# A long convolution's 16-point stages on row halves of the systolic array, and one output stored from another queue

## The chip, the cores and the metric

The kernel runs on one NeuronCore of a Trainium2 chip. The core has TensorE (PE, the 128x128 systolic array, which writes only to PSUM), VectorE (DVE), ScalarE (ACT), GpSimd (POOL) and SyncE (SP); SP, ACT and POOL also issue DMAs, each in its own order. The metric is the device time of one execution, in microseconds, the median of several. Whatever is called a weight load (PEld) is the loading of a matmul's stationary operand; the moving operand then streams through the array, one column after the other.

## The reference

The program computes a network of four residual layers on x = A_q (2048 positions, 448 channels) and the gradients of everything.

- Layer A, used twice: `x + n * (conv(kv) + kv * D)`, where n is the layer norm of x, `kv = shift(k) * v` with a causal 4-tap shift, and conv is a causal convolution of 2048 positions with one kernel per channel, which the reference does with an FFT of 4096 points.
- Layer B, used twice: `x + silu(norm(x) @ w1) @ w2`, with 1792 hidden units.
- The outputs: the result, and the gradients by A_q, k, v, the shift kernel, the long kernel (448x2048), D, w1 and w2. All in bf16.

kv does not depend on x, so the convolution is done once forwards, and its backward pass once, with the gradient that both layers A leave.

## The kernel before

**The convolution.** A position is n = 16 n1 + n2. Stage 1 is, for each of the 16 values of n2, a pair of matmuls (real and imaginary part) with a 128x128 table over n1 (`_fft_stage1`, line 198). Its result A1 has, for each frequency k1 on a partition, blocks of 128 columns, which hold 4 channels x 2 parts x 16 values of n2. Each block is transposed on TensorE (`turn`, line 350; line 1091 in the backward part), so that these 128 values lie on the partitions. Stage 2 (`_fft_stage2`, line 206) multiplies by a 128x128 matrix that holds a 16-point transform for each of the 4 channels. In the spectrum the product of two complex numbers is taken by two real products on DVE, one with a copy in which real and imaginary half have changed places (`_swap_halves` on DVE, `_swap_halves_dma` by two DMAs). The inverse (`_fft_inv_stage2_chunk`, line 216) takes a chunk of 8 blocks: for each block two matmuls of 128x128 by 128 columns, accumulated; this also turns the block back. Last, matmuls with the inverse table give the positions (lines 496, 1173, 1202). A spectrum has 14 chunks of 1024 columns, worked in pairs; "cp" counts the seven pairs.

**The order.** `_ssm_prefix` does the spectrum of the long kernel (K), then the convolution of kv: from about 5 to 101 us. K's spectrum stays on chip as `KAB` with its swapped copy, and is also stored to DRAM (`SPEC_d`), as is that of kv. `Main.run` does the layers forwards and backwards, in four blocks of 512 positions, to about 517 us. `_ssm_suffix` does the convolution's backward pass: stage 1 on the gradient (`_s1_gy`), the transposes, then `spectrum(cp)` and `inverse(cp)` in turn, each inverse twice, for the gradients of the kernel (`B1k`) and of kv (`B1v_`); then the gradients of v and k, the kernel gradient `gK` (lines 1194 to 1206) and that of the shift kernel (lines 1218 to 1233).

**Jobs.** The weight gradients of layer B are 56 products of 16 matmuls with 448 moving columns (class `Jobs`, line 950), cut into 224 steps of four matmuls. `jobs.run(n)` puts n steps into TensorE's program at that place. They fill TensorE while other engines prepare the next part of the convolution. `jobs.run(1000)` at the end does what is left; a result's transposes and store come one result later (`flush`, line 1028).

**What sets the order.** TensorE's order is the program's, by hand (`manual_schedule`). For the other engines a planner of the framework orders the instructions by its own estimates. `bal.pick` gives each eviction from PSUM to ACT or DVE by a running sum of estimated loads. PSUM is used in tagged rings: "mm" has two buffers of two banks in the main and backward part, "A" four such buffers in the prefix. The products `pa`, `pb` of the backward inverse lie in a ring of three (`pab`); `gK` has two buffers.

Of the kernel before, what the change touches and what calls it, by code (L numbers as in the profile page):

```python
# [17 lines left out]
P = 128  # L18
S = 2048
D = 448  # L20
# [8 lines left out]
NDH = D // 4  # L29
SPEC = NDH * P  # L30
# [3 lines left out]
def make_fft_consts():  # L34
# [10 lines left out]
    def qidx(m, c, ks):  # L45
        return 64 * c + 4 * m + ks
# [32 lines left out]
    GiBc = np.roll(GiBc, 64, axis=0)  # L79
# [118 lines left out]
def _fft_stage1(k, n2, rhs, A1, psum, m=None):  # L198
    nc = k.nc
    ps = psum.tile([P, 2, 512], FP32, name="ps_s1", **k.pt["s1"])  # L200
    for c in range(2):
        nc.tensor.matmul(ps[:, c, :D], lhsT=k.M1sb[:, n2 if m is None else m, c, :], rhs=rhs, start=True, stop=True)
    _copy(nc, k.bal.pick(2 * D), A1[:, :, :, n2, :].rearrange("p dh c ds -> p c dh ds"), ps[:, :, :D].rearrange("p c (dh ds) -> p c dh ds", ds=4))


def _fft_stage2(k, Zf, psum, consume, chunks, base=0):
    nc = k.nc
    for ci in chunks:
        ps = psum.tile([P, 1024], FP32, name="ps_s2", **k.pt["s2"])
        for hh in range(2):  # L210
            c0 = (ci - base) * 1024 + hh * 512
            nc.tensor.matmul(ps[:, hh * 512:(hh + 1) * 512], lhsT=k.Gsb[:, G_FWD, :], rhs=Zf[:, c0:c0 + 512], start=True, stop=True)
        consume(ci, ps)


def _fft_inv_stage2_chunk(k, pa, pb, conj, B1, ci, psum, cnd=False):
    nc = k.nc
    ga, gb = (G_IAC, G_IBC) if conj else (G_IA, G_IB)
    pv = psum.tile([P, 8, P], FP32, name="ps_v", **k.pt["v"])
    for i in range(8):  # L220
        nc.tensor.matmul(pv[:, i, :], lhsT=pa[:, i * P:(i + 1) * P], rhs=k.Gsb[:, ga, :], start=True, stop=False)  # L221
        nc.tensor.matmul(pv[:, i, :], lhsT=pb[:, i * P:(i + 1) * P], rhs=k.Gsb[:, gb, :], start=False, stop=True)  # L222
    if cnd:
        _copy(nc, k.bal.pick(1024), B1[:, :, 32 * ci:32 * ci + 32].rearrange("p q (dh ds) -> p dh q ds", ds=4),
              pv[:].rearrange("p dh (q ds) -> p dh q ds", ds=4))
    else:
        _copy(nc, k.bal.pick(1024), B1[:, 8 * ci:8 * ci + 8, :].rearrange("p a b -> p (a b)"), pv[:].rearrange("p a b -> p (a b)"))
# [7 lines left out]
def _swap_halves_dma(k, dst, src, lo, hi, eng, dlo=None):  # L235
    if dlo is None:
        dlo = lo
    dhi = dlo + (hi - lo)
    eng.dma_start(out=dst[0:64, dlo:dhi], in_=src[64:128, lo:hi])
    return eng.dma_start(out=dst[64:128, dlo:dhi], in_=src[0:64, lo:hi])  # L240
# [46 lines left out]
def _ssm_prefix(k):  # L287
# [4 lines left out]
    with ExitStack() as es:  # L292
# [8 lines left out]
        A1kv = k.mdp.tile([P, NDH, 2, 16, 4], BF16, name="A1kv", tag="DA")  # L301
        KAB = spec.tile([P, 2, SPEC], BF16, name="KAB")
        A1K = KAB[:, 0, :].rearrange("p (a c n s) -> p a c n s", c=2, n=16, s=4)
# [46 lines left out]
        def turn(src, dst, g):  # L350
            pt = psum.tile([P, 16, P], BF16, name="ps_tr", **a_)
            for i in range(16):
                nc.tensor.transpose(pt[:, i, :], src[:, 16 * g + i, :], k.ident[:])  # L353
            for lo, hi, o in dst(g):
                _copy(nc, bal.pick((hi - lo) * P, dve_ns=0.53), o, pt[:, lo:hi, :])
# [35 lines left out]
        def stage1_kv(h, jq, kvt):  # L391
            for u in range(0, 4, 2):
# [5 lines left out]
                for w in range(2):  # L398
                    _copy(nc, bal.pick(2 * DH), A1kv[:, 56 * h:56 * (h + 1), :, n2 + w, :].rearrange("p dh c ds -> p c dh ds"),
                          ps[:, w, :, :DH].rearrange("p c (dh ds) -> p c dh ds", ds=4))  # L400

        def cons_ka(ci, ps):
            sl = slice(ci * 1024, (ci + 1) * 1024)
            _copy(nc, bal.pick(1024), Ka[:, sl], ps[:])
            if ci % 2 == 1:
                lo, hi = (ci - 1) * 1024, (ci + 1) * 1024
                nc.gpsimd.dma_start(out=k.SPEC_d["K"][:, lo:hi], in_=Ka[:, lo:hi])
# [6 lines left out]
        for h in range(2):  # L414
            for i, jq in enumerate((1, 2, 3, 0)):
# [9 lines left out]
                else:  # L425
                    _fft_stage2(k, Ka, psum, cons_ka, range(2 * i, 2 * i + 2))
                    _swap_halves_dma(k, KAB[:, 0, :], Ka, 2048 * i, 2048 * i + 2048, nc.gpsimd)
# [6 lines left out]
        _fft_stage2(k, Ka, psum, cons_ka, range(8, NCI))  # L434
        for i in range(4, 7):
            _swap_halves_dma(k, KAB[:, 0, :], Ka, 2048 * i, 2048 * i + 2048, nc.gpsimd)

        B1 = A1kv[:].rearrange("p a c n s -> p a (c n s)")
# [8 lines left out]
        A1f = A1kv[:].rearrange("p a c n s -> p a (c n s)")  # L447
        for g in range(7):
            turn(A1f, zdst, g)
# [32 lines left out]
        for ci in range(NCI):  # L482
            _fft_stage2(k, zkv(ci * 1024, (ci + 1) * 1024), psum, cons_prod, (ci,), ci)
# [3 lines left out]
        B1v = B1.rearrange("p a (c n s) -> p a c n s", c=2, n=16)  # L487
        k.Ysb = k.wk.tile([P, J, D], BF16, name="Ysb", tag="W2")

    def ys():  # L490
        for i in range(8):
            py = k.psum.tile([P, 2, 512], FP32, name="ps_y", tag="mm", bufs=2)
            for u in range(2):
                n2 = 2 * i + u
                for c in range(2):
                    nc.tensor.matmul(py[:, u, :D].rearrange("p (dh ds) -> p dh ds", ds=4), lhsT=k.Minvsb[:, n2, c, :], rhs=B1v[:, :, c, n2, :], start=(c == 0), stop=(c == 1))
# [9 lines left out]
class Main:  # L506
# [257 lines left out]
    def run(self, ys):  # L764
# [57 lines left out]
        for c in range(4):  # L822
# [59 lines left out]
            else:  # L882
# [5 lines left out]
                k.A1g = k.mdp.tile([P, NDH, 2, 16, 4], BF16, name="A1g", tag="DA")  # L888
# [161 lines left out]
def _ssm_suffix(k):  # L1050
# [8 lines left out]
    with ExitStack() as es:  # L1059
# [28 lines left out]
        for g in range(7):  # L1088
            pt = psum.tile([P, 16, P], BF16, name="ps_tr", **mm)
            for i in range(16):  # L1090
                nc.tensor.transpose(pt[:, i, :], A1f[:, 16 * g + i, :], k.ident[:])
# [185 lines left out]
```

## Time and profile before

| what | time or share |
|---|---|
| runs before: median of 3 | 728.43 us (728.0 to 730.16) |
| the profiled execution's own time | 730.31 us |
| its span in the trace | 728.5 us |
| PE busy | 690.6 us, 95% |
| DVE busy | 472.7 us, 65% |
| ACT busy | 444.8 us, 61% |
| POOL busy | 98.1 us, 13% |
| inverse chunks, lines 221 and 222: matmuls | 336 + 336 |
| stage 2, lines 212 and 1103: matmuls | 56 + 28 |
| transposes, lines 353 and 1091: matmuls | 192 + 112 |

A row of the timeline gives the start, the length, the engine, the line, and how many equal instructions it joins; in brackets, how long the engine had been idle and what released it. The length of a joined row reaches from the first start to the last end, and ends of matmuls are modelled: a single matmul of 448 columns lasts 353 ns, but in a stream the next starts after 190 ns. So paces are taken from starts, and busy time per instruction is no pace. A row of the windows gives the start and end of the stretch, its length, then for PE, PEld, DVE, ACT and POOL the busy time and in brackets the instructions, then TensorE's granted clock, the busy share of the DMA engines and their GB/s.

### The profile page before, as it was taken

The numbers are of one execution on the slowest core, as the hardware profiler recorded it, in microseconds if no ns is written. First come the engines' busy times: TensorE is split into PE (matmuls) and PEld (weight loads), VectorE is DVE, ScalarE is ACT, GpSimd is POOL, SyncE is SP. The second block draws the span as 40 slices with busy tenths as digits, with TensorE's granted clock in tenths as the row PEclk, the third lists the DMA queues.
The fourth block names the chain that finished last, engine by engine and source line by source line (L and its number), as shares of the span: only waits on it lengthen the run. The fifth ranks groups of instructions, "written<-read, shape, count | busy, mean of one in ns | idle before, by whom it ended". The sixth has DMA issues, their size and how long they took to land.

```text
span 728.5 us, 12878 instructions
## 1 busy us (share of the span) xinstructions
PE 690.6 (95%) x5105; PEld 383.8 (53%) x5105; DVE 472.7 (65%) x1112; ACT 444.8 (61%) x545; POOL 98.1 (13%) x165
## 2 busy tenths in 40 slices
PE   6998799899999999999999999999899999999897
PEld 4876545454544444444444444545466666655654
DVE  4789843666879658898488845836764444449930
ACT  5888774578988858778587792135354445444311
POOL 1153110110010100101001000000102110013221
PEclk9999999999999999999999999999999999999999
DMA  9999946279939897197881999787648896568861
GB/s 316 261 286 327 373 110 167 91 175 258 273 108 223 227 237 195 48 242 229 229 205 38 228 249 345 190 215 191 228 159 328 302 358 242 155 185 275 292 211 48
DMA packets 192905, 160.64 MB, mean 220 GB/s; under 512 B 140619, under 2 KB 173134, under 8 KB 191948
## 3 DMA queue, kind: packets, MB, share of 16 engines
q1 hardware_dynamic: 178240, 111.14, 57.2%
q0 software_dynamic: 10896, 38.58, 15.1%
q10 hardware_dynamic: 3708, 10.09, 3.8%
q8 instruction: 40, 0.66, 0.4%
q14 instruction: 21, 0.17, 0.1%
HBM read 67.32 MB, written 54.60 MB: 167 GB/s over the span
## 4 chain that ended last, share of the span: by engine, by line
PE 65%; DVE 13%; issue 10%; ACT 7%; POOL 2%; DMA 2%; SPq 0%; DVEq 0%; ACTq 0%; POOLq 0%
PE ps_d L950 20%; PE ps_n L737 9%; PE ps_h L565 7%; PE ps_g L565 7%; PE ps_o L699 6%; PE ps_v L221 2%; PE ps_v L222 2%; POOL rstd L260 2%; PE ps_h L569 1%; PE ps_cv L381 1%; PE ps_g L569 1%; DVE n L262 1%; DVE pab L475 1%; PE ps_tr L353 1%; ACT KAB L111 1%
## 5 line engine op out<-in xcount | busy, mean ns | idle before, releaser
L950 PEld LDWEIGHTS <-dstat 128*128 128x128 bf16 x896 | 85.0, 98 | 73.5 <-issue 2.4
L737 PE MATMUL ps_n<-w1T,ghT 128*128 128x448 bf16 x448 | 95.0, 353 | 0.0
L699 PE MATMUL ps_o<-w2sb,aT 128*128 128x448 bf16 x448 | 89.9, 353 | 2.5 <-DVE X L703 2.5
L565 PE MATMUL ps_h<-nT,w1sb 128*128 128x512 bf16 (+1 forms) x420 | 84.8, 337 | 4.1 <-ACT Dall L111 2.4
L565 PE MATMUL ps_g<-nT,w2T 128*128 128x512 bf16 x336 | 79.7, 379 | 1.1 <-DVE Dall L112 0.6
L111 ACT CAST ghT<-ps_g 128x1024 bf16<-128x1024 f32 (+1 forms) x54 | 47.8, 903 | 53.3 <-PE ps_g L569 38.7
L737 PEld LDWEIGHTS <-ghT 128*128 128x128 bf16 x448 | 41.6, 98 | 44.6 <-issue 7.9
L699 PEld LDWEIGHTS <-aT 128*128 128x128 bf16 x448 | 43.0, 98 | 42.0 <-issue 5.0
L565 PEld LDWEIGHTS <-w1sb 128*128 128x128 bf16 x420 | 39.2, 98 | 40.4 <-issue 11.5
L682 ACT ACTIVATE aT<-ps_h 128x1024 bf16<-128x1024 f32 (+1 forms) x48 | 44.2, 921 | 20.6 <-PE ps_h L569 12.3
L898 DVE SCALAR_TENSOR_TENSOR lb_v<-lb_u,n 128x448 bf16<-128x448 bf16 x60 | 37.3, 621 | 28.9 <-ACT lb_u L741 28.4
L111 ACT CAST Dall<-ps_h 128x1024 bf16<-128x1024 f32 (+2 forms) x60 | 54.3, 904 | 0.0
L692 ACT ACTIVATE Dall<-Dall 128x1024 bf16<-128x1024 bf16 (+1 forms) x48 | 53.8, 1189 | 0.1
L565 PEld LDWEIGHTS <-w2T 128*128 128x128 bf16 x336 | 31.8, 98 | 38.2 <-issue 4.9
L260 POOL TENSOR_TENSOR rstd<-ln_ve,mhalf 128x2 f32<-128x2 f32 (+1 forms) x24 | 19.3, 805 | 222.9 <-DVE ln_ve L259 213.1
L950 PE MATMUL ps_d<-X,dstat 128*128 128x448 bf16 x224 | 48.4, 352 | 0.0
L950 PE MATMUL ps_d<-go,dstat 128*128 128x448 bf16 x224 | 48.1, 353 | 0.0
L950 PE MATMUL ps_d<-n3m,dstat 128*128 128x448 bf16 x224 | 48.1, 357 | 0.0
L950 PE MATMUL ps_d<-n1m,dstat 128*128 128x448 bf16 x224 | 47.3, 355 | 0.0
L221 PE MATMUL ps_v<-Gsb,pab 128*128 128x128 bf16 x336 | 42.2, 219 | 5.4 <-DVE pab L475 5.3
L222 PE MATMUL ps_v<-Gsb,pab 128*128 128x128 bf16 x336 | 42.0, 219 | 1.2 <-DVE pab L1117 1.2
L221 PEld LDWEIGHTS <-pab 128*128 128x128 bf16 x336 | 32.7, 98 | 11.6 <-DVE pab L475 8.2
(205 smaller groups left out, 1154.7 us busy)
## 6 DMA issues: line engine op xcount, KB each, us to landing
dstat<-a_d SPq DMA_DIRECT2D x28, 512.0 KB, 4.6
dstat<-g_d SPq DMA_DIRECT2D x28, 512.0 KB, 4.4
a_d<-turned SPq DMA_DIRECT2D x16, 512.0 KB, 3.2
g_d<-turned SPq DMA_DIRECT2D x16, 512.0 KB, 2.9
a_d<-turned SPq DMA_DIRECT2D x16, 384.0 KB, 2.9
g_d<-turned SPq DMA_DIRECT2D x16, 384.0 KB, 2.6
spec_K<-KAB POOLq DMA_DIRECT2D x7, 512.0 KB, 7.6
KAB<-KAB POOLq DMA_DIRECT2D x14, 256.0 KB, 8.5
```

Of the source, the lines that this page charges most:

```text
L111: return nc.scalar.copy(out, in_)
L221: nc.tensor.matmul(pv[:, i, :], lhsT=pa[:, i * P:(i + 1) * P], rhs=k.Gsb[:, ga, :], start=True, stop=False)
L222: nc.tensor.matmul(pv[:, i, :], lhsT=pb[:, i * P:(i + 1) * P], rhs=k.Gsb[:, gb, :], start=False, stop=True)
L260: nc.gpsimd.tensor_tensor(out=r[:, lo:hi], in0=ve[:, lo:hi], in1=k.mhalf[:, lo:hi], op=ALU.pow)
L565: self.nc.tensor.matmul(ps, lhsT=w[:, b, ft * P:(ft + 1) * P], rhs=x[:, b], start=(start and b == 0), stop=(stop and b == bs[2]))
L569: self.nc.tensor.matmul(ps, lhsT=w[sl, b, ft * P:(ft + 1) * P], rhs=x[sl, b], start=start, stop=stop)
L682: self.last_silu = nc.scalar.activation(aT[hh][:, o:o + hi - lo, :], ps[:, lo:hi, :], ACT.Silu)
L692: self.nc.scalar.activation(dT[hh][:, o:o + n, :], dT[hh][:, o:o + n, :], ACT.Derivative_silu)
L699: nc.tensor.matmul(po[:, :D], lhsT=aT[ft // 7][:, ft % 7, tl * P:(tl + 1) * P], rhs=self.w2sb[:, ft, :], start=(ft == 0), stop=(ft == NF - 1))
L737: nc.tensor.matmul(pn[:, :D], lhsT=gh[ft // 7][:, ft % 7, tl * P:(tl + 1) * P], rhs=self.w1T[:, ft, :], start=(ft == 0), stop=(ft == NF - 1))
L898: nc.vector.scalar_tensor_tensor(out=v[:], in0=u0, scalar=-1.0 / D, in1=n_t, op0=ALU.mult, op1=ALU.mult, accum_out=cp[:, 1:2])
L950: self.nc.tensor.matmul(ps[:, :D], lhsT=st[:, t, :], rhs=mov[:, t, :], start=(first and t == 0), stop=(last and t == NT - 1))
```

## The change

The blocks of 128 columns are laid out anew: instead of 64 values of the real part and 64 of the imaginary (`64 * c + 4 * m + ks`) a block has two halves of 64, each with two whole channels (`64 * (ks // 2) + 32 * c + 2 * m + ks % 2`). The 128x128 matrices of the 16-point stages then are two blocks of 64x64 on the diagonal. Each of these matmuls is replaced by matmuls on one half of the array's rows: a transpose by two of 64 rows and 64 columns, an inverse matmul likewise, into PSUM tiles whose two halves are different banks, and stage 2 by 64x64 tiles, for a pair of chunks at once. Chunks of odd number have their two halves exchanged by that, which the inverse undoes. The half swap becomes four pieces of 32 partitions. In A1 the innermost run has 2 elements rather than 4, and so has all that reads or writes it. Stage 2 works on pairs, so the order of stage 2, evictions and jobs changes a little in each place, and in the backward inverse both products' chunks follow each other, with `jobs.run(6)` behind them in place of `jobs.run(3)` behind each. Besides, the kernel gradient is stored by a DMA from ACT's queue instead of POOL's.

```diff
-        return 64 * c + 4 * m + ks
+        return 64 * (ks // 2) + 32 * c + 2 * m + ks % 2
...
-    GiBc = np.roll(GiBc, 64, axis=0)
+    GiBc = GiBc[np.arange(128) ^ 32]
...
-    _copy(nc, k.bal.pick(2 * D), A1[:, :, :, n2, :].rearrange("p dh c ds -> p c dh ds"), ps[:, :, :D].rearrange("p c (dh ds) -> p c dh ds", ds=4))
+    _copy(nc, k.bal.pick(2 * D), A1[:, :, :, n2, :].rearrange("p b c s -> p c b s"), ps[:, :, :D].rearrange("p c (b s) -> p c b s", s=2))
+
+
+def _turn64(k, pt, i, src):
+    for r in range(2):
+        rs = slice(64 * r, 64 * r + 64)
+        k.nc.tensor.transpose(pt[:, r, i, :], src[rs], k.ident[rs, rs])
...
-def _fft_stage2(k, Zf, psum, consume, chunks, base=0):
+def _fft_stage2(k, Zf, psum):
     nc = k.nc
-    for ci in chunks:
-        ps = psum.tile([P, 1024], FP32, name="ps_s2", **k.pt["s2"])
-        for hh in range(2):
-            c0 = (ci - base) * 1024 + hh * 512
-            nc.tensor.matmul(ps[:, hh * 512:(hh + 1) * 512], lhsT=k.Gsb[:, G_FWD, :], rhs=Zf[:, c0:c0 + 512], start=True, stop=True)
-        consume(ci, ps)
+    ps = [psum.tile([P, 1024], FP32, name="ps_s2", **k.pt["s2"]) for _ in range(2)]
+    for hh in range(2):
+        o = slice(hh * 512, hh * 512 + 512)
+        for f in range(2):
+            for r in range(2):
+                ri, ro = slice(64 * r, 64 * r + 64), slice(64 * (r ^ f), 64 * (r ^ f) + 64)
+                nc.tensor.matmul(ps[f][ro, o], lhsT=k.Gsb[ri, G_FWD, ri], rhs=Zf[f][ri, o], start=True, stop=True)
+    return ps
...
-    pv = psum.tile([P, 8, P], FP32, name="ps_v", **k.pt["v"])
+    pv = psum.tile([P, 2, 8, 64], FP32, name="ps_v", **k.pt["v"])
     for i in range(8):
-        nc.tensor.matmul(pv[:, i, :], lhsT=pa[:, i * P:(i + 1) * P], rhs=k.Gsb[:, ga, :], start=True, stop=False)
-        nc.tensor.matmul(pv[:, i, :], lhsT=pb[:, i * P:(i + 1) * P], rhs=k.Gsb[:, gb, :], start=False, stop=True)
+        for src, g, first in ((pa, ga, True), (pb, gb, False)):
+            for r in range(2):
+                ri = slice(64 * r, 64 * r + 64)
+                nc.tensor.matmul(pv[:, r ^ (ci & 1), i, :], lhsT=src[ri, i * P:(i + 1) * P], rhs=k.Gsb[ri, g, ri], start=first, stop=not first)
...
+SWAPS = [(slice(64 * h + 32 * c, 64 * h + 32 * c + 32), slice(64 * h + 32 - 32 * c, 64 * h + 64 - 32 * c)) for h in range(2) for c in range(2)]
...
 def _swap_halves(k, dst, src):
-    k.nc.vector.tensor_copy(dst[0:64], src[64:128])
-    return k.nc.vector.tensor_copy(dst[64:128], src[0:64])
+    for o, i in SWAPS:
+        last = k.nc.vector.tensor_copy(dst[o], src[i])
+    return last
...
+def _swap_halves_dma(k, dst, src, lo, hi):
+    for o, i in SWAPS:
+        k.nc.gpsimd.dma_start(out=dst[o, lo:hi], in_=src[i, lo:hi])
...
-            pt = psum.tile([P, 16, P], BF16, name="ps_tr", **a_)
+            pt = psum.tile([P, 2, 16, 64], BF16, name="ps_tr", **a_)
             for i in range(16):
-                nc.tensor.transpose(pt[:, i, :], src[:, 16 * g + i, :], k.ident[:])
+                _turn64(k, pt, i, src[:, 16 * g + i, :])
...
-        for ci in range(NCI):
-            _fft_stage2(k, zkv(ci * 1024, (ci + 1) * 1024), psum, cons_prod, (ci,), ci)
+        for cp in range(NCI // 2):
+            cis = (2 * cp, 2 * cp + 1)
+            for ci, ps in zip(cis, _fft_stage2(k, [zkv(ci * 1024, (ci + 1) * 1024) for ci in cis], psum)):
+                cons_prod(ci, ps)
...
         def spectrum(cp):
             xsw = _hd(k, [P, 2048], "xsw_c")
             kk = kks[cp]
-            for u in range(2):
-                ps = psum.tile([P, 1024], FP32, name="ps_s2", **mm)
...
-                k.last_x = nc.scalar.copy(Zf[cp][:, u * 1024:(u + 1) * 1024], ps[:])
-                jobs.run(1)
+            zs = [Zf[cp][:, u * 1024:(u + 1) * 1024] for u in range(2)]
+            for z, ps in zip(zs, _fft_stage2(k, zs, psum)):
+                k.last_x = nc.scalar.copy(z, ps[:])
+            jobs.run(3)
             _swap_halves(k, xsw, Zf[cp])
...
-                for spec_t, B1, cnd in ((t[1], B1k, True), (t[0], B1v_, False)):
+                prods = []
+                for spec_t in (t[1], t[0]):
                     pa, pb = pab[:, 0, n_p[0] % 3], pab[:, 1, n_p[0] % 3]
...
+                    prods.append((pa, pb))
+                for (pa, pb), B1, cnd in zip(prods, (B1k, B1v_), (True, False)):
                     _fft_inv_stage2_chunk(k, pa, pb, True, B1, ci, psum, cnd=cnd)
-                    jobs.run(3)
+                jobs.run(6)
...
-            nc.gpsimd.dma_start(out=out5v[:, dc, :], in_=gK[:])
+            nc.scalar.dma_start(out=out5v[:, dc, :], in_=gK[:])
```

The transposes at line 1091 and the other users of A1 are changed in the same way; the spectrum of K in the prefix is also worked in pairs, each followed by its store and its four swap DMAs.

More of the change, by code (lines that the diff above doesn't have):

```diff
@@ L29 @@
 NDH = D // 4
+NB = D // 2
 SPEC = NDH * P
@@ L887, in run @@
                     k.m1h.append(m)
-                k.A1g = k.mdp.tile([P, NDH, 2, 16, 4], BF16, name="A1g", tag="DA")
+                k.A1g = k.mdp.tile([P, NB, 2, 16, 2], BF16, name="A1g", tag="DA")
                 k.pt = dict(s1=dict(tag="mm", bufs=2))
@@ L1088, in _ssm_suffix @@
         for g in range(7):
-            pt = psum.tile([P, 16, P], BF16, name="ps_tr", **mm)
+            pt = psum.tile([P, 2, 16, 64], BF16, name="ps_tr", **mm)
             for i in range(16):
-                nc.tensor.transpose(pt[:, i, :], A1f[:, 16 * g + i, :], k.ident[:])
-            _copy(nc, bal.pick(2048, dve_ns=0.53), Z[g], pt[:])
+                _turn64(k, pt, i, A1f[:, 16 * g + i, :])
+            _copy(nc, bal.pick(2048, dve_ns=0.53), Z[g].rearrange("p i (r x) -> p r i x", r=2), pt[:])
             jobs.run(1)
```

57 lines of the change are left out of this document (23 added, 34 removed).

## The prediction

> **What bounds the kernel now.** I read the page first, then busy time by window, then the timeline of the stages that the diff touches.
>
> ```profile
> PE 690.6 (95%) x5105; PEld 383.8 (53%) x5105; DVE 472.7 (65%) x1112; ACT 444.8 (61%) x545; POOL 98.1 (13%) x165
> ...
> 60.00:70.00 10.00, 8.44 (x123) 7.00 (x121) 8.56 (x9) 8.21 (x9) 4.03 (x8) 1.00 1.04 350
> 70.00:80.00 10.00, 8.34 (x109) 6.15 (x107) 9.37 (x9) 9.73 (x11) 2.15 (x4) 1.00 1.02 370
> 540.00:550.00 10.00, 8.81 (x81) 5.63 (x79) 7.92 (x13) 4.15 (x5) 1.63 (x3) 1.00 0.85 312
> 560.00:570.00 10.00, 10.00 (x89) 6.46 (x87) 4.94 (x8) 3.96 (x5) 1.67 (x4) 1.00 0.79 277
> 680.00:690.00 10.00, 7.87 (x59) 4.94 (x58) 10.00 (x15) 4.05 (x7) 2.45 (x5) 0.83 0.73 242
> ```
>
> The columns are time, length, then PE, weight loads, DVE, ACT, POOL, the granted clock and the DMA share. The touched work lies in two places with different limits. From 57 to 90 us (first convolution) DVE and ACT are over 80% busy and PE waits for products. From 550 to 720 us (backward convolution with weight-gradient jobs between its parts) PE is full, but for a dip near 685. There a microsecond of PE is a microsecond of time. The period of one spectrum pair shows it: 14 job steps of 4x189.7 ns, four inverse chunks of 0.89 and four stage-2 matmuls of 0.216 add up to 15.06 us, and the chain of waits repeats every 15.03 (543.87, 558.90, 573.93).
>
> ```profile
> 130.27 0.39 PE L569 MATMUL ps_g<-nT,w2T 64*128 64x512 bf16 x2
> 130.59 1.47 PE L565 MATMUL ps_g<-nT,w2T 128*128 128x512 bf16 x6
> 131.99 0.39 PE L569 MATMUL ps_g<-nT,w2T 64*128 64x512 bf16 x2
> ...
> 524.98 1.06 PE L1091 MATMUL ps_tr<-ident,A1g 128*128 128x128 bf16 x16
> 525.87 0.92 PE L950 MATMUL ps_d<-X,dstat 128*128 128x448 bf16 x4
> ...
> 684.96 1.01 ACT L1203 CAST gK<-ps_gK 112x1024 bf16<-112x1024 f32 x1 [6.57 <-DMA out_dram<-gK]
> 686.02 1.48 PE L1202 MATMUL ps_gK<-Minvs,A1g 128*112 128x128 bf16 x16 [2.13 <-ACT gK L1203]
> ...
> 700.01 1.68 PE L950 MATMUL ps_d<-n3m,dstat 128*128 128x448 bf16 x8
> 701.61 1.08 PE L1224 MATMUL ps_sk<-kx_s,gks 128*32 128x128 bf16 x64
> 702.62 1.69 PE L950 MATMUL ps_d<-n3m,dstat 128*128 128x448 bf16 x8
> ```
>
> Three prices come from these lines. (1) *Tiles run side by side.* The two 64-row matmuls of line 569 end 0.39 us after the first starts, and one alone lasts 383 ns: both stream together. Line 1224 runs four 32-column tiles into one PSUM bank; 64 matmuls start within 1.08-0.22 = 0.86 us, so four cost 56 ns, and about 14 ns per load-and-matmul is issued. (2) *A change of tile mode costs 0.10 us.* Six matmuls from 130.59 end streaming at 130.59+6x0.216 = 131.89, the 64-row pair starts at 131.99; after 0.216 of streaming from 130.27 the full-array work resumes at 130.59. In and out is 0.2 us. (3) *Pace is linear in columns.* 448 columns: (1.68-0.35)/7 = 190 ns; 128: (1.06-0.219)/15 = 56; 112 (line 381, 32 in 1.74): 49. That is 0.418 ns a column plus 2.5. No row has 64; the line gives 29.2 ns.
>
> **The parts.** All is summed against the profiled execution: 730.3 us, of which the span is 728.5. It stands 1.9 above the median of 728.4, so the result is moved down by 1.9.
>
> *Inverse chunks (lines 221, 222).* 16 matmuls of 128 columns become 16 pairs of 64-row tiles with 64 columns. Before 16x55.8 = 0.89 us. Bounds after: 0.47 (29.2 ns a pair) and 0.89 (56 ns: short streams gain nothing). I take 0.47: a pair asks for one load-and-matmul per 14.6 ns, which line 1224 nearly shows, and each half writes its own bank, as at line 569; the 64x128 loads last 94 ns against 98 for 128x128, so they are the fast kind. In the backward part both chunks of a half-step now follow each other, one excursion for two: 28x0.43 saved, 14x0.2 paid, -9.1 us (at the other end +2.8).
>
> *Stage 2 (line 1103).* Per pair of chunks four matmuls of 512 columns become eight 64x64 ones, four at a time: 0.86 to 0.43, an excursion 0.2, seven times: -1.6 us. Other end: nothing overlaps, 1.73, +7.5. I take the first; line 1224 shows four tiles with separate moving data and one bank, in separate partitions. The Trainium skill (TensorEngine Tiling (Array Packing), Gotcha 1: PSUM Pressure) says that different row tiles cannot use one PSUM bank at once, and here tiles (0,0) and (1,1) do. By that rule two of four would run together, and the sum would be 3.0 us worse; no run here has row tiles in one bank.
>
> *Transposes (line 1091).* Seven groups, 0.89 to 0.47, each with an excursion: -1.6 us (other end +1.4).
>
> *Kernel gradient stored from ScalarE.* POOL issues the first stores at 678.96, after a wait for a DVE product, though the first gK was ready at 673.6. The buffer (two of them) is late, ACT waits 6.57 us, PE 2.13. The clock then falls: the 16 matmuls at 686.02 and the eight job matmuls behind them take 4.1 us instead of 2.4. From ACT the store is issued at 673.6 and lands 5.8 us later, before 682.4, when the buffer is wanted. -3.9 us. ACT pays four issues (0.35 each at line 1185) at 40% busy; behind them wait its own gK copies, which two PSUM buffers and two job steps cover. What is late next is DVE, full to 697.6, whose masks at 702.74 had 5.2 us of slack; 1.3 is left.
>
> *Order of jobs.* A spectrum pair is followed by three job steps, not two of one. Seven steps move ahead, so the 224 run out inside the last fixed call instead of six after it: the matmuls of line 1239, their copy and two POOL issues then come after the last flush: +0.7 us (0 to 1.5).
>
> *Half swaps.* Four 32-partition copies for two of 64: 2x0.689 us more, seven times, 9.6 us of DVE. Windows 550 to 620 have DVE at 4 to 5 of 10, and the ring of three product buffers lets it run ahead; steady state hides it. The start does not: around 540 PE already waits 1.2 us for a product; now products wait for 1.4 us more of swap, both PSUM tiles must be free for a stage-2 pair, and the second chunk has no jobs before it, so the second swap (2.8 us) may be in front of its product. 0 to +4, I take +2. As DMAs, 14 more issues of 0.52 us put 7.3 us on POOL between 43 and 70; spectrum stores queue behind them. The last swap would be issued near 69 and land 8.5 later; its product is due near 85.
>
> *First convolution.* On PE: turning K in three excursions, 5x0.43-0.6 = -1.5; stage 2 of K -0.2 each; turning KV 7x0.43. But evictions there allow one turned group per 0.74 us (1.87 on ACT, 1.22 on DVE), and from 63 to 90 DVE and ACT set the pace. -2 us, between -4 and +2 (pairs may upset the alternation).
>
> *Layout.* Innermost runs of two elements instead of four. ACT writes runs of four in 907 ns (A1g) against 917 packed (Ysb), and moving reads of such runs take 350 ns against 353 packed, so: nothing. Upper end from the only single-element read, the weights of line 340, 99 ns a matmul instead of 49: +0.2 us for each of 64 matmuls of lines 496 and 1173, +12.8.
>
> Sum: -9.1-1.6-1.6-3.9+0.7+2-2 = -15.5 us: 714.8 for a profiled execution, 712.9 against the median.
>
> **Rivals.**
> *A. Slower: weight loads no longer hide.* A 64-row tile must be reloaded every 29 ns; if its load waits for its own stream, a pair costs more than the 56 of a full-array matmul. 35 chunks and groups of 16 pairs lie in the full PE stretch, so each ns of pace is 0.56 us; with the other terms the break-even is at 29.2+15.5/0.56 = 57 ns a pair. With p = 80: 560x51 ns = +28.4 on the forecast, 741, before the first convolution adds its share. Against it: full-array transposes reload the same rows every 56 ns with 98 ns loads under the stream. The Trainium skill (TensorE: Matmul & The Clock Gate, Part 3, The mechanism) says that loads overlap running matmuls only where the row group differs; the rows of line 1091 speak against that rule. Chance 0.17.
> *B. Short streams gain nothing* (56 ns a pair): the suffix pays excursions for stage 2 alone, +14.9 on the forecast: 728. Partial: 35 to 50 ns, 716 to 725. For it: no row under 112 columns. Chance 0.13 in all, 0.05 of it within the bound.
> *C. Two-element runs slow moving reads*: 713+12.8 = 726 at most; half of that, 719, if only partly. Line 340 shows the effect for single elements, none for four. The Trainium skill (SBUF — State Buffer, Door 1: The DMA port swizzle, its note on 16-byte cachelines) asks for two hits a line, which a run of two just gives. Chance 0.08.
> *D. PE gains but waits*: DVE, with 9.6 us more, is late in every period rather than once: it would have to lose over 1 us a period, +7 to 8: 721. Against: 4 to 5 of 10 busy. Chance 0.07.
>
> **How the numbers follow.** The forecast has 0.55; its own range is 707 (prefix -4, no start cost, and -2 where pairs relieve evictions) to 718 (start +4, prefix +1). A change under 0.3% (2.2 us) cannot be told here. Faster: 0.55+0.08 of B+0.08+0.07 = 0.78; same 0.05; slower 0.17. The range runs from 706 to 730: A lies outside, B, C and D inside.
>
> **What would show it.** Right: line 222's successor starting pairs under 35 ns apart, 64x64 sets of four within 0.24 us, a spectrum period (15 steps) near 14.3 us, no wait of ACT for gK's store, clock 1.00 at 680. Wrong: pairs at 56 ns or more, moving reads of ps_gkv over 400 ns, PE waits on products at each half-step, or a last stage where DVE's masks are late.

## The result, and the profile after

The changed kernel takes 736.98 us (median; 735.77 to 738.13), the kernel before 729.29 in the same session (728.0 to 730.68). The ratio is 1.0106, with a 95% interval of 1.0078 to 1.0133: slower by about 8 us, where 713.0 was forecast. The profiled execution has a span of 736.3 us, against 728.5.

The page's busy times, then five windows (those shown of before), then rows of the timeline:

```profile
PE 685.3 (93%) x6165; PEld 359.1 (49%) x6165; DVE 481.5 (65%) x1126; ACT 444.9 (60%) x545; POOL 102.7 (14%) x175
...
60.00:70.00 10.00, 5.78 (x216) 3.59 (x211) 8.16 (x9) 7.86 (x8) 7.21 (x14) 1.00 1.02 321
70.00:80.00 10.00, 6.21 (x208) 3.93 (x207) 9.80 (x10) 10.00 (x12) 4.28 (x10) 1.00 0.97 311
540.00:550.00 10.00, 9.24 (x166) 4.54 (x158) 4.50 (x6) 5.98 (x5) 0.55 (x1) 1.00 0.32 110
560.00:570.00 10.00, 10.00 (x116) 5.17 (x114) 2.59 (x5) 2.50 (x3) 2.76 (x4) 0.98 0.72 254
680.00:690.00 10.00, 10.00 (x86) 6.29 (x85) 9.69 (x15) 3.94 (x6) 3.37 (x5) 1.00 0.87 292
```

```profile
549.57 0.63 PE L221 MATMUL ps_s<-B1v,Gsb 64*64 64x512 bf16 x8
...
563.84 1.11 PE L233 MATMUL ps_v<-Gsb,pab 64*128 64x64 bf16 x64
...
696.05 1.01 ACT L1215 CAST gK<-ps_gK 112x1024 bf16<-112x1024 f32 x1 [2.23 <-DMA out_dram<-gK]
```

TensorE did become cheaper. The 64 inverse matmuls at 563.84 take 1.11 us, a single one 0.19: 0.92/63 = 14.6 ns each, 29.2 a pair, as forecast. Eight 64x64 matmuls of stage 2 take 0.63, a single one 0.40 by the profile: the second set of four starts 0.24 us after the first. But from 60 to 80 us TensorE's busy time has fallen from 16.8 to 12.0 us and the stage did not become shorter: POOL, in its place, went from 6.2 to 11.5.

Starts of some events (timeline, by tile; us), with the fastest version of the experiments beside them:

| event | before | after | fastest version |
|---|---|---|---|
| convolution's last stage, first `ps_y` | 90.5 | 93.8 | 90.6 |
| main part, first `ps_h` | 103.5 | 111.4 | 105.4 |
| backward transposes, first | 525.0 | 535.4 | 528.5 |
| backward stage 2, first | 536.5 | 545.5 | 538.6 |
| period of a spectrum pair | 15.03 | 14.30 | 13.55 |
| `ps_gkv`, first to last | 643.9-666.4 | 653.2-681.5 | 639.6-662.0 |
| `gK`, first to last | 668.8-690.9 | 684.2-702.3 | 664.5-682.6 |
| end of the span | 728.5 | 736.3 | 720.5 |

So 7.9 us are lost by the start of the main part: 3.3 before the first `ps_y`, and 4.6 behind it (17.6 us to the main part instead of 13.0). A period gains 0.73 us although it holds 15 job steps instead of 14 (the fastest version has 14 again, and gains 1.48). The stage of `ps_gkv` grows from 22.5 to 28.3 us, and `gK` shrinks from 22.1 to 18.1.

### The profile page after: what moved, and what is told of

The parts are those of the page before. It is cut to its first block, busy times and chain, and to the rows that moved or that the text cites. A ratio compares the mean times of both kernels' runs of the same rounds, so it can differ in the third digit from the quotient of the medians.

```text
span 736.3 us, 15043 instructions
## 1 busy us (share of the span) xinstructions
PE 685.3 (93%) x6165; PEld 359.1 (49%) x6165; DVE 481.5 (65%) x1126; ACT 444.9 (60%) x545; POOL 102.7 (14%) x175
## 4 chain that ended last, share of the span: by engine, by line
PE 60%; DVE 13%; DMA 10%; issue 8%; ACT 5%; POOL 2%; SPq 1%; POOLq 0%; ACTq 0%; DVEq 0%
PE ps_d L962 22%; PE ps_n L749 7%; PE ps_h L577 6%; PE ps_g L577 5%; PE ps_o L711 4%; DMA KAB<-KAB 2%; DMA spec_K<-KAB 2%; PE ps_v L233 2%; DMA turned<-aT 2%; PE ps_y L508 2%; PE ps_gkv L1185 2%; POOL rstd L272 2%; PE ps_h L581 1%; DMA go<-in_grad_out_dram 1%; DVE n L274 1%
## 5 line engine op out<-in xcount | busy, mean ns | idle before, releaser
L962 PEld LDWEIGHTS <-dstat 128*128 128x128 bf16 x896 | 84.9, 99 | 82.5 <-issue 11.5
L577 PEld LDWEIGHTS <-w1sb 128*128 128x128 bf16 x420 | 39.2, 98 | 40.4 <-issue 11.5
L962 PE MATMUL ps_d<-n3m,dstat 128*128 128x448 bf16 x224 | 46.6, 353 | 0.0
L233 PE MATMUL ps_v<-Gsb,pab 64*128 64x64 bf16 x1344 | 26.9, 196 | 15.2 <-DVE pab L485 8.1
L557 ACT COPY nT<-ps_t 128x1024 bf16<-128x1024 bf16 x28 | 28.1, 1010 | 17.1 <-PE ps_t L556 17.0
L246 DVE COPY xsw_c<-B1v 32x2048 bf16<-32x2048 bf16 x28 | 19.2, 685 | 26.3 <-ACT B1v L1113 26.0
```

Source lines behind the costliest of these rows:

```text
L233: nc.tensor.matmul(pv[:, r ^ (ci & 1), i, :], lhsT=src[ri, i * P:(i + 1) * P], rhs=k.Gsb[ri, g, ri], start=first, stop=not first)
L246: last = k.nc.vector.tensor_copy(dst[o], src[i])
L557: nc.scalar.copy(dst[:rows, 2 * h:2 * h + 2, :], pt[:rows])
L577: self.nc.tensor.matmul(ps, lhsT=w[:, b, ft * P:(ft + 1) * P], rhs=x[:, b], start=(start and b == 0), stop=(stop and b == bs[2]))
L962: self.nc.tensor.matmul(ps[:, :D], lhsT=st[:, t, :], rhs=mov[:, t, :], start=(first and t == 0), stop=(last and t == NT - 1))
```

## The experiments

All times are medians; ratios are to the kernel before on the same chip, with 95% intervals.

**1. The layout.** The evictions of the inverse write the 32 channels of a chunk next to each other, so that `ps_y` and `ps_gkv` read runs of 32 elements instead of two.

```diff
-    _copy(..., B1[:, 8 * ci:8 * ci + 8, :].rearrange("p i (h x) -> p h i x", h=2), pv[:])
+    _copy(..., B1[:, 8 * ci:8 * ci + 8, :]....rearrange("p (q i h s) -> p h i q s", i=8, h=2, s=2), pv[:].rearrange("p h i (q s) -> p h i q s", s=2))
...
-    rhs=B1v[:, :, c, n2, :]
+    rhs=B1v[:, :, 16 * c + n2, :]      # in ps_y and in ps_gkv
```

> The changed kernel, but the inverse chunks are evicted in another order inside their 1024 columns (part and n2 outermost, then 32 channels), so that the last matmuls of the convolution read runs of 32 elements instead of 2; evictions then write runs of two, as those of the kernel gradient do. Theory S (two-element runs double the moving read: 0.19 us becomes 0.38 for 64 matmuls): both groups fall to 350 ns in length and 0.19 us in pace, 32x0.19 = 6.1 us goes in the backward part and 4 to 6 in the first convolution, 724 to 727 us. Rival Q (the loss is the DMA queue and products that come late, the slow reads lie beside these waits): under 4 us goes, 733 to 736.

Measured: 727.83, ratio 0.9985 (0.9963 to 1.0007). This edit alone takes back what the change lost (the time is close above theory S, 724 to 727, and far from rival Q). Groups of the kernel before and of the changed one (count | busy time, mean ns of one | idle time before, and what ended it):

```profile
L1173 PE MATMUL ps_gkv<-B1v,Minvs 128*128 128x448 bf16 x32 | 7.4, 350 | 0.0
L496 PE MATMUL ps_y<-A1kv,Minvsb 128*128 128x448 bf16 x32 | 6.9, 350 | 2.9 <-DVE A1kv L112 1.4 <-ACT Ysb L111 1.2 <-ACT ghT L111 0.2
```

```profile
L1185 PE MATMUL ps_gkv<-B1v,Minvs 128*128 128x448 bf16 x32 | 13.4, 551 | 0.0
L508 PE MATMUL ps_y<-A1kv,Minvsb 128*128 128x448 bf16 x32 | 12.6, 555 | 1.4 <-DVE A1kv L113 1.4
```

With two-element runs a matmul lasts 0.55 us instead of 0.35, and the pace doubles: 16 of `ps_y` from 98.47 take 6.23 us, (6.23-0.56)/15 = 0.38 instead of 0.19. 64 matmuls by 0.19 are 12 us, of which the prefix hides a part. With runs of 32, `ps_gkv` takes 22.4 us again. The gain in the prefix can't be read from that profile, whose own execution took 732.27, 4.4 above the median: VectorE waits 5.9 us there for swap transfers, `ps_y` starts only at 99.1 and the main part at 113.6, later than in the changed kernel.

**2. What counts in a read.** In the kernel before, the matmuls of line 1173 read 448 columns in eight patterns, one for each group of four; w@s means runs of w elements every s. That kernel leaves out the right gradients of v, k and the shift kernel, and was run once (734.19); only the pace of the matmuls is read from it.

```diff
-    rhs=B1vv[:, :, c, n2, :]
+    w, s = ((1, 32), (1, 2), (2, 64), (2, 8), (2, 4), (4, 128), (4, 8), (8, 256))[i]
+    rhs=f[:, 0:448 // w * s].rearrange("p (b s) -> p b s", s=s)[:, :, 0:w]
```

> The kernel before, but the 32 matmuls of line 1173 read the right number of columns (448) in eight other patterns, one for each of the eight groups of four, so the gradients of v, k and the shift kernel are not computed rightly; the work is the same. Written as run length at distance, in elements of two bytes: 1 at 32, 1 at 2, 2 at 64, 2 at 8, 2 at 4, 4 at 128, 4 at 8, 8 at 256. Theory S as a matter of 16-byte lines (a line must be hit by at least two pairs): slow (0.38 us a matmul) are 1 at 32, 2 at 64 and 2 at 8; 0.19 us are 1 at 2, 2 at 4, 4 at 128, 4 at 8 and 8 at 256. Rival, a matter of the run's length alone: every run of two and one is slow, also 2 at 4 and 1 at 2.

The timeline, in the order of the patterns:

```profile
646.61 3.16 PE L1176 MATMUL ps_gkv<-B1v,Minvs 128*128 128x448 bf16 x4
...
652.10 0.95 PE L1176 MATMUL ps_gkv<-B1v,Minvs 128*128 128x448 bf16 x4
...
655.16 1.67 PE L1176 MATMUL ps_gkv<-B1v,Minvs 128*128 128x448 bf16 x4
...
658.95 1.75 PE L1176 MATMUL ps_gkv<-B1v,Minvs 128*128 128x448 bf16 x4
...
663.02 0.95 PE L1176 MATMUL ps_gkv<-B1v,Minvs 128*128 128x448 bf16 x4
...
666.08 0.92 PE L1176 MATMUL ps_gkv<-B1v,Minvs 128*128 128x448 bf16 x4
...
669.33 0.95 PE L1176 MATMUL ps_gkv<-B1v,Minvs 128*128 128x448 bf16 x4
...
672.39 0.92 PE L1176 MATMUL ps_gkv<-B1v,Minvs 128*128 128x448 bf16 x4
```

Single elements at distance 32 take 3.16 us for four matmuls, but at distance two 0.95, the full rate. Runs of two at 64 and at 8 take 1.67 and 1.75, at 4 again 0.95, and the three patterns with runs of four and eight 0.92 to 0.95. From start to start that is 0.75 us a matmul for single elements, 0.38 to 0.40 for two at 64 and at 8, and 0.19 for the rest. It is not the length of the run, but how many wanted elements lie in 16 bytes (eight elements of bf16): four or more give the full rate, two half of it, one about a quarter. Pieces of 32 bytes do not fit these rows (two at 8 would have four elements in each, as four at 128 have), nor do pieces of 8 (two at 8 would be no worse than single ones at 2). The Trainium skill (SBUF — State Buffer, Door 1: The DMA port swizzle, the note on 16-byte cachelines) asks for two hits a line. By these rows one bf16 element is no such hit: four elements were needed for the full rate. The same note's "8 bf16" as a stride that is free does not hold for these reads: two of every eight run at half rate.

**3. The swap transfers of the prefix.** Alone in the kernel before (each of the 14 transfers cut in two, all on POOL), and in the changed kernel with every second one issued by SP.

```diff
-    eng.dma_start(out=dst[0:64, dlo:dhi], in_=src[64:128, lo:hi])
-    return eng.dma_start(out=dst[64:128, dlo:dhi], in_=src[0:64, lo:hi])
+    for o in range(0, 128, 32):
+        i = (o + 64) % 128
+        last = eng.dma_start(out=dst[o:o + 32, dlo:dhi], in_=src[i:i + 32, lo:hi])
```

> The kernel before with its 14 swap DMAs of 256 KB cut into 28 of 128 KB, all from POOL, nothing else. Theory Q: POOL waits for DMAs eight back, the last swaps start near 80 instead of 65, DVE waits 2 to 3 us for them, and the whole is 2 to 5 us slower, 731 to 734. Rival (the bytes are the same, and the products are due late enough): within 0.5 us of the kernel before.

```diff
-    for o, i in SWAPS:
-        k.nc.gpsimd.dma_start(out=dst[o, lo:hi], in_=src[i, lo:hi])
+    for n, (o, i) in enumerate(SWAPS):
+        (k.nc.gpsimd, k.nc.sync)[n % 2].dma_start(out=dst[o, lo:hi], in_=src[i, lo:hi])
```

> The changed kernel, but every second of the 28 swap DMAs of K's spectrum is issued from SP, so POOL issues 14 as before the change. Theory Q (a POOL DMA starts only when the one eight issues before it has landed, so 14 more of them make the swapped spectrum late for the products on DVE): POOL's waits for DMAs in that stretch fall from some 18 us to under 4, DVE's wait of 2.8 us for the swapped spectrum is gone, the first matmul of the main part comes 3 to 5 us earlier, 732 to 734. Rival: the DMA engines, busy all the time there, are the limit, and the queue does not matter: 736 to 737.

Measured: the cut alone 735.56, ratio 1.0094 (1.0077 to 1.0110), 7 us for an item that the prediction costed at nothing; `ps_y` starts at 97.5, the main part at 110.5. With SP's help the changed kernel takes 734.34, ratio 1.0086 (1.0058 to 1.0114), not clearly better than without (1.0106), and between the ranges of theory and rival; together with runs of 32 it takes 726.64:

> The changed kernel with two repairs: runs of 32 elements and half of the swap DMAs from SP, jobs as in the change. If the queue hid part of the first repair's gain (there the products waited 5.2 us for a swap DMA), the two together give 12 us and more: 722 to 725. Rival: each gives no more than alone: 725.5 to 728.

Ratio 0.9973 (0.9957 to 0.9990), again close to experiment 1. POOL's rows of the changed kernel:

```profile
53.08 0.51 POOL L252 DMA_DIRECT2D KAB<-KAB  x1 [5.92 <-DMA KS_d<-ks_kv]
55.58 0.49 POOL L252 DMA_DIRECT2D KAB<-KAB  x1 [1.99 <-DMA spec_K<-KAB]
...
81.00 0.49 POOL L252 DMA_DIRECT2D KAB<-KAB  x1 [0.65 <-DMA KAB<-KAB]
```

POOL's issue costs 0.5 us, but before it POOL waits for an older transfer of its own to land: in these programs the one eight issues earlier, counted back along its queue. The kernel before had 5.2 us of such waits between 40 and 82 us, in nine places, a sign that the prediction passed over; the changed kernel has 15 us. With 14 more issues the last swap leaves POOL at 81.00 (65.50 before) instead of the "near 69" of the prediction, and VectorE waits 3.0 us for a swap. With every second swap on SP, POOL's last one is issued at 71.14 and VectorE waits for none, but the main part starts only 1.9 us earlier (109.5). By this run the late queue accounts for about 2 of the 7.9 us.

The cut alone costs its 7 us in another way than theory Q said. There POOL waits only 3.1 us for its own transfers, its last swap is issued at 71.70 and landed at 80.08, and VectorE waits for no swap. Instead VectorE's copies and products of the last chunks stand in another order, and it waits 5.0 us in all for stage 2 of TensorE. The longest of these waits:

```profile
87.83 1.22 DVE L112 CAST ZkvB<-ps_s 128x1024 bf16<-128x1024 f32 x1 [3.43 <-PE ps_s L212]
```

TensorE in turn waits twice 2.45 us for products there, and its granted clock is 0.76 from 85 to 90 us and 0.66 from 90 to 95. In the kernel before, the copy in this place follows three products and waits for nothing:

```profile
80.97 3.48 DVE L475 TENSOR_TENSOR pab<-ZkvB,KAB 128x2048 bf16<-128x2048 bf16 x3
84.38 1.22 DVE L112 CAST ZkvB<-ps_s 128x1024 bf16<-128x1024 f32 x1
```

That the planner chose another order for a program with more transfers is the reading that fits. No run kept the order and cut the transfers alone, so the cause of these 7 us stays open.

**4. VectorE's half swap alone.** In the kernel before, the swap of the last stage is cut into four copies of 32 partitions.

```diff
-    k.nc.vector.tensor_copy(dst[0:64], src[64:128])
-    return k.nc.vector.tensor_copy(dst[64:128], src[0:64])
+    for o in range(0, 128, 32):
+        i = (o + 64) % 128
+        last = k.nc.vector.tensor_copy(dst[o:o + 32], src[i:i + 32])
```

> The kernel before, with one part of the change alone: VectorE's half swap of the last stage is cut into four copies of 32 partitions (0.70 us each by the changed kernel's rows: 2.79 for four) in place of two of 64 partitions (1.40 for both). If the backward inverse's start costs the changed kernel time because VectorE swaps twice as long before the second chunk's products (PE waited 0.76 + 0.92 + 2.88 us there), then two swaps add 2 x 1.4 = 2.8 us at the start and nothing in the steady state: 730.5 to 731.5. Rival: the start hides it, or VectorE's extra 1.4 us in each of seven periods of 15 us costs every time: 728.4, or 738.

Measured: 734.62, ratio 1.0091 (1.0073 to 1.0109): 6.7 us, more than twice the theory's 2.8. The wait of TensorE at the start of the backward inverse, in the kernel before and with the cut swap:

```profile
542.86 0.23 PE L222 MATMUL ps_v<-Gsb,pab 128*128 128x128 bf16 x1 [1.19 <-DVE pab L1117]
```

```profile
541.29 5.59 DVE L233 COPY xsw_c<-B1v 32x2048 bf16<-32x2048 bf16 x8
...
547.66 0.26 PE L222 MATMUL ps_v<-Gsb,pab 128*128 128x128 bf16 x1 [4.79 <-DVE pab L1119]
```

Both swaps run back to back, 5.59 us, before the first swapped product: 3.6 us more of waiting. The granted clock then is 0.77 from 545 to 550 and 0.89 from 550 to 555 (1.00 before), at most another 1.7. By 562 us that profile is 6.5 us behind that of the kernel before, so some 5 us are lost at this start, and 2 are regained by the end of the span (733.0 against 728.5). The periods behind it stay at 15.03 us (stage 2 at 561.93, 576.96, 591.99), so the steady state does hide the swap. The prefix of that profile is 1.3 us later too, which the edit does not explain. The changed kernel's longest wait at the same start:

```profile
557.14 0.98 PE L233 MATMUL ps_v<-Gsb,pab 64*128 64x64 bf16 x30 [2.88 <-DVE pab L1127]
```

**5. The order of jobs at that start.** In the changed kernel, two job steps behind a spectrum instead of three, and four steps between the first two chunks.

```diff
-            jobs.run(3)
+            jobs.run(2)
             _swap_halves(k, xsw, Zf[cp])
...
                     _fft_inv_stage2_chunk(k, pa, pb, True, B1, ci, psum, cnd=cnd)
+                    if ci == 0 and cnd:
+                        jobs.run(4)
-                jobs.run(6)
+                jobs.run(6 if cp else 4)
```

> The changed kernel with another order of the jobs only: two steps behind a stage-2 pair instead of three, so that six or seven are left for the end as before, and at the very first inverse four steps between the two chunks and four behind. Theory: the stall at 552 to 558 (3.8 us of PE waiting for products behind two half swaps) shrinks to under 1.5, and the gradient of the shift kernel no longer is stored last, the tail of 7.6 us after the last job's first matmul falls to 5.2; together 731.5 to 733. Rival: PE waits elsewhere for the same DVE work, 735 to 737.

Measured: 736.19, ratio 1.0092 (1.0061 to 1.0123), no clear difference from the changed kernel. The tail behind the last weight-gradient matmul is 5.4 us again, as in the kernel before (5.2; changed kernel 7.6), but TensorE is busy only 5.63 us of 550 to 560: jobs do not help where VectorE's swaps stand in the way. All three repairs together:

> The changed kernel with the three repairs together: runs of 32 elements for the last matmuls, half of the swap DMAs from SP, and the other order of the jobs. If the three losses are separate, the parts add: about 737 less 12 for the reads, less 2.6 for the queue, less 4.5 for the jobs: 718 to 721. Rival: the first convolution is bound by DVE and ACT and takes back what the reads give there: 722 to 725.

Measured: 726.58, ratio 0.9974 (0.9958 to 0.9991). That is above both expectations and not clearly better than the layout alone (0.9963 to 1.0007): the repairs do not add.

**6. The second swap later, and the transposes of the prefix whole.** Both start from that version. One moves VectorE's second swap behind the first pair's products; the other undoes the split of the prefix's transposes; the third run does both.

```diff
-            _swap_halves(k, xsw, Zf[cp])
+            if cp != 1:
+                _swap_halves(k, xsw, Zf[cp])
...
+                if ci == 1:
+                    _swap_halves(k, cur[2], Zf[1])
```

> The version with runs of 32, SP swaps and fewer jobs, with VectorE's second half swap of the last stage moved behind the products of the first chunk pair's second half (it is needed one period later). Theory: PE's wait of 4.4 us for VectorE's product at the start of the backward inverse (548.5 in that version) shrinks to 1.6 or less, total 723.5 to 724.5. Rival: the wait only moves to the second pair's products, total 726 to 727.

```diff
-                _turn64(k, pt, i, src[:, 16 * g + i, :])
+                nc.tensor.transpose(pt[:, i, :], src[:, 16 * g + i, :], k.ident[:])
```

> The version with runs of 32, half of the swap transfers on SP and fewer jobs at the start (726.6), with the convolution's transposes of the prefix whole again: 16 of 128x128 in place of 32 of 64x64 a group, the same output. The split kernels show PE idle for nothing that the profile names, 2.2 to 3.8 us, always after the 166th of the last 224 transposes (near 60.5), and in that stretch a 16 KB packet of the instruction queue is being moved while the 16 DMA engines are busy 1.04 of the time. Theory (PE's instructions arrive late because the split doubles their number for the same work): the gap goes, ps_y starts about 2 us earlier (90 in place of 92.1), total 724 to 726. Rival (the gap is something else, or is hidden behind the evictions of ACT and VectorE and the swap transfers): the gap stays or ps_y's start stays, total 726 to 728, the whole transposes being 0.3 us a group longer.

> Both of the two edits before this one together: whole transposes in the prefix and the late second swap. If both theories hold and add, 721 to 723; if only one holds, 724 to 726; if neither, 726 to 728.

Measured: late swap 722.01, ratio 0.9918 (0.9898 to 0.9937), TensorE's wait 2.2 us instead of 4.4; whole transposes 724.66, ratio 0.9946 (0.9930 to 0.9961), `ps_y` at 90.0; both 720.51, ratio 0.9897 (0.9882 to 0.9913). That is the fastest version, 7.4 us below the kernel before. The late swap's gain is clear; that of the whole transposes is not, as its interval overlaps the one without them in both pairs of runs. TensorE's wait at the start, with the late swap:

```profile
546.59 0.61 PE L233 MATMUL ps_v<-Gsb,pab 64*128 64x64 bf16 x30 [2.17 <-DVE pab L1129]
```

In the changed kernel the 224 transposes of the prefix stop after 166 (timeline), and in the microsecond where they stop the list of DMA queues shows one packet of instructions, 0.02 MB, which takes 8.3% of the 16 engines' time, 1.3 us:

```profile
59.87 0.73 PE L210 MATMUL ps_tr<-ident,A1kv 64*128 64x64 bf16 x38 [0.20 <-ACT ZkvA L112]
62.98 1.02 PE L210 MATMUL ps_tr<-ident,A1kv 64*128 64x64 bf16 x58 [2.38 <-issue]
```

```profile
q0 software_dynamic: 76, 0.25, 96.6%
q8 instruction: 1, 0.02, 8.3%
```

With whole transposes they run through:

```profile
57.36 6.43 PE L366 MATMUL ps_tr<-ident,A1kv 128*128 128x128 bf16 x112
```

The stop stands behind the same transpose in seven of the eight profiles with split transposes (the one of experiment 1 stops 2.6 us after 38 and 0.6 again after 166), and with whole ones it is gone. That TensorE waits for its own program there would fit, but it is not shown: the trace does not say for which engine the packet was, and packets of the same queue also pass during the whole transposes of the kernel before (at 61.9 us) and of the two versions here (59.4 and 58.9) without a stop.

**7. The store of the kernel gradient.** Alone in the kernel before (on ACT), then undone in the changed kernel and in the fastest version (on POOL).

```diff
-            nc.gpsimd.dma_start(out=out5v[:, dc, :], in_=gK[:])
+            nc.scalar.dma_start(out=out5v[:, dc, :], in_=gK[:])
```

> The kernel before with one part of the change alone: the kernel gradient is stored from ACT. As in the prediction: PE's wait of 2.1 us near 684 and the slow clock behind it go, -3.9 us: 724.5 to 725.5. Rival (DVE, full until 697.6, is next and takes the gain back): -1 to -2.

> The changed kernel with one part undone: the kernel gradient is stored from POOL again. In the kernel before, the move to ACT by itself gave nothing (0.7 per mille), yet in the changed kernel the gK stage takes 18.1 us instead of 22.1 and TensorE does not wait in it. Theory (the move pays there, because ACT's queue meets the store at once and the transfer is over when the buffer is wanted): with POOL the stage is 20 us or more again and TensorE waits about 2 us for ACT's copy; 3 to 4 us slower than the changed kernel: 740 to 741. Rival (the stage is shorter because it lies elsewhere in the traffic of the load jobs, whoever issues): 736.5 to 737.5.

> The fastest version so far (runs of 32, SP swaps, fewer jobs at the start, whole transposes in the prefix, late second swap: 720.5), with the kernel gradient stored from POOL. Theory that ACT's queue makes the difference: 723.5 to 724.5 and a wait of TensorE in the gK stage; rival: 720 to 721.

Measured: alone 728.67, ratio 1.0007 (0.9995 to 1.0019): nothing. Undone in the changed kernel 738.15, ratio 1.0148 (1.0110 to 1.0185, against 1.0078 to 1.0133 with the store on ACT); undone in the fastest version 722.67, ratio 0.9913 (0.9889 to 0.9937, against 0.9882 to 0.9913). Each interval overlaps the one it is compared with, and 738.15 lies between the two expectations, but both traces say the same of the stage: the `gK` stage is 20.1 and 20.4 us long instead of 18.1 in each, and TensorE waits 1.8 and 2.1 us again. The run of the store alone:

```profile
675.39 0.34 ACTq L1205 DMA_DIRECT2D out_dram<-gK  x1
...
685.12 1.01 ACT L1203 CAST gK<-ps_gK 112x1024 bf16<-112x1024 f32 x1 [6.28 <-DMA out_dram<-gK]
```

There ACT issued the store only behind its next copy, 1.4 us after the data was ready, and it took 9.7 us to land, beside the loads of `kx_s` that ACT had issued at 667 and with the DMA engines busy 98% of 670 to 680. In the fastest version it landed within 7.5 us (670.65 to 678.13), just early enough for TensorE not to wait.

**8. The granted clock in the prefix.** In the fastest version each stage-2 matmul of the prefix is issued twice.

```diff
-        for f in range(2):
+        for f in [0, 1] * rep:       # rep = 2 in the prefix
```

> The same fastest version, with each stage-2 matmul of the prefix issued twice (14 sets of eight, 0.43 us more for each, 6 us of TensorE in all, in a stretch where it is 60 to 80% busy; the output is the same). It shows what the fallen granted clock costs there (0.50 to 0.87 between 70 and 94 us). Theory (the gate halves the clock because TensorE idles, and this delays the convolution): the clock stays near 1.00, the main part starts up to 2 us earlier than 105.4, total 718.5 to 720. Rival (the evictions and the swap transfers set the pace, the clock costs nothing that counts): 720 to 722 at about the same start; and if TensorE's extra work is on the path, up to 726.

Measured: 725.73, ratio 0.9947 (0.9928 to 0.9966), half a per cent slower than without; the main part starts at 109.3 instead of 105.4. The clock did not stay up (0.77, 0.71 and 0.66 in the three windows of 8 us from 78). So the extra work was on the path, and no run separates what the lower clock by itself costs. A trace at hand shows it for one place, in the fastest version and in the kernel before:

```profile
90.58 3.14 PE L509 MATMUL ps_y<-A1kv,Minvsb 128*128 128x448 bf16 x8 [1.41 <-DMA w2sb<-in_B_w_dram]
```

```profile
90.52 1.68 PE L496 MATMUL ps_y<-A1kv,Minvsb 128*128 128x448 bf16 x8 [1.41 <-DVE A1kv L112]
```

The same eight matmuls take 3.14 us where the granted clock is 0.50 (90 to 94) and 1.68 where it is 1.00; the next eight take 2.25 (0.70 from 94 to 98) against 1.68. Together that is 2.0 us, and the fastest version, whose `ps_y` starts at the same time, starts the main part 1.9 us later.

## Why the prediction was wrong, step by step

- **"Inverse chunks", "stage 2", "transposes": right.** 29.2 ns a pair, 0.24 us for a set of four, 14.30 us for a period of 15 steps ("near 14.3"), and in the fastest version a period of 13.55 instead of 15.03 with the same 14 job steps: 7x1.48 = 10.4 us against 9.1+1.6. Rivals A and B fell. The Trainium skill (TensorEngine Tiling (Array Packing), Gotcha 1: PSUM Pressure) would have made a set of four two after two; the rows say that both row halves worked on one bank at once.
- **"Layout ... so: nothing": wrong, the largest error.** The step took four-element and packed rows as the nearest, and they lie at the full rate (0.19 us); two elements lie on the other side of an edge and take 0.38. Its own upper end of 12.8 was nearly the raw cost (64 by 0.19 = 12 us), and 1.21% of the time, 8.8 us, came back by experiment 1. Rival C, with a chance of 0.08, was the right mechanism, but it too subtracted only this and would have left the kernel faster.
- **"As DMAs, 14 more issues ... due near 85": wrong.** The sum has no term for them. The step counted POOL's issue time and a landing time, not POOL's waits for its own transfers, which grew from 5.2 to 15 us: the last swap was issued at 81.0, and VectorE waited 3.0 us. That is about 2 us of the time by the run with SP's help. The cut alone costs 7 us, though its transfers land in time (80.08); there the order of VectorE's work differs, and the cause stays open.
- **"Half swaps ... 0 to +4, I take +2": the mechanism right, the size too small.** TensorE waited 0.92+2.88 us for products at 553 to 557. The part alone costs 6.7, beyond the range; the late second swap gave back 4.
- **"First convolution -2": the wrong sign.** The step saw that DVE and ACT set the pace there, and still gave TensorE's savings a gain. The prefix became 7.9 us longer: two-element reads of `ps_y` and late swaps are parts of it that rows and runs price, the rest stays open. Even the fastest version starts the main part 1.9 us later than before, with `ps_y` at a granted clock of 0.50 and 0.70.
- **"Kernel gradient ... -3.9": about half, and only with the rest.** Alone nothing; in the changed kernel about 2 us of the stage. The step kept the 5.8 us landing of POOL's store for another queue and time.
- **"Order of jobs +0.7 (0 to 1.5)": small.** The tail grew by 2.4 us, and undoing it changed the total by too little to tell.

Two losses were foreseen at nothing and one at two. The costs of the parts alone (7 and 6.7) and the layout's 9 add up to more than the 8 us lost, because TensorE's gain covers some of them. They are not independent either: the layout, half the swaps on SP and the jobs repaired together gave no more than the layout alone. That a late prefix hides another delay in it would explain this, but was not tested. One difference was not followed up: from the start of the main part to the backward transposes the changed kernel takes 424.0 us instead of 421.5, with a wait of 1.0 for a product of the gradient's stage 1 and evictions into runs of two at 940 ns instead of 907.

## What to carry to other kernels

When a matmul is made cheaper by a new layout, price every other reader of that layout first: for TensorE's moving operand count the elements in each 16 bytes. Cutting a VectorE copy along the partitions keeps each piece as long as the whole (0.70 us for 32 partitions, 0.69 for 64), and cutting a transfer doubles the issues. The places to look are the start of a pipeline, where nothing hides it, the queue that issues them, and the order of work that the planner makes of it. A gain that is right by itself (10 us here) shows only once those are repaired.

## What the runs showed of the hardware

- Moving reads: 0.19 us per 448 columns with four or more bf16 elements in 16 bytes, 0.37 to 0.40 with two, about 0.75 with one.
- Row-tile matmuls of 64 columns keep the linear pace of longer ones, 14.6 ns for each load and matmul, two at a time.
- In these programs a DMA is issued by POOL only when the one eight issues earlier has landed (waits of up to 5.92 us).
- In seven of eight profiles TensorE stops for 2.2 to 3.8 us behind the 166th of 224 short transposes, with no releaser in the trace, while a 16 KB packet of instructions moves through busy DMA engines; with 112 whole ones there is no stop. The cause is not shown.
- In the changed kernel the granted clock fell to 0.57 and 0.50 in two windows of 4 us from 82 in which TensorE was busy 1.27 and 1.13 us, and stayed at 0.50 for 8 us more although TensorE was busy again; in the kernel before it was 1.00 throughout the prefix.
